# Windowed attention and a cosine MLP in one kernel: double bursts, a late division in the first chunk, and dues shifted by part

## The chip, the cores and the metric

The kernel runs on one core of a Trainium2 chip. A core has five engines that run side by side, each through its own list of instructions: TensorE (PE, with its weight loads shown as PEld), VectorE (DVE), ScalarE (ACT), GpSimd (POOL) and SyncE (SP, which issues the DMAs). They wait for each other by semaphores. The metric is the device time of one execution in microseconds (us); lower is better. Before the change the median of three runs is 677.84 us (677.83 to 678.22).

## The reference

Inputs are `q`, `k`, `v` of 4 batches, 8 heads, 768 positions, 64 numbers a head; a token sees the 96 positions up to itself and the first 8 (global) ones, with a bias that falls linearly with the distance at a slope of its head. The result goes through a two-layer network with `h * cos(h)` between.

```python
scores = scale * np.matmul(q, k.transpose(0, 1, 3, 2))
...
dist = np.where(is_global & ~is_local, float(n_local), np.abs(rel).astype(np.float32))
slopes = 2.0 ** (-8.0 * (np.arange(H, dtype=np.float32) + 1) / H)
scores = np.where(keep, scores - slopes * dist, -1e9)        # per head
a = np.exp(scores - np.max(scores, axis=-1, keepdims=True))
a = a / (np.sum(a, axis=-1, keepdims=True) + 1e-09)
x = np.matmul(a, v)                                          # 3072 tokens x 512
...
h = x @ w_in                                                 # 512 x 2048
return ((h * np.cos(h)) @ w_out).astype(np.float32)          # 2048 x 512
```

`w_in` and `w_out` arrive as 8-byte numbers and are taken apart on the chip into a high and a low 4-byte part; products of the network are made of three matmuls (high by high, low by high, high by low).

## The kernel before, in words

Work comes in chunks. Chunks 0 and 1 are the two halves of batch 0, four blocks of 96 positions each (OPEN). Batches 1 to 3 have three chunks each (BLOCKS): two of three blocks and one of two, chunks 2 to 10. Each chunk has four units, one for each pair of heads (UB is 1, so `plan_unit` and `plan_values` deal with one pair at a time).

A unit goes like this. Scores on PE (L678 where the unit is "exact", the eight units of chunks 0 and 1; L682 elsewhere) go into a PSUM bank. DVE folds two masked pieces into one (L700) and then, in one instruction for each block and head (L709), adds the distances `dd`, scales and keeps the maximum. ACT takes the exponential and its sum (L734). DVE adds 1e-9 and inverts the sums (L742, L745). POOL or DVE multiplies the probabilities by that inverse (`norm`, L762 and L767). PE turns them (L866), DVE and ACT copy them to `pv` (L877, L883, L310), and a burst of small matmuls (L917) multiplies them by the values into a bank `px`: each matmul writes one half of the partitions, a half for each head of the pair. Then `plan_x` copies `px` to the high part of x (`high`, L310 or L312) and subtracts for the low part (`rest`, L965). In an exact unit the queries are scaled by a factor of the head first (`queries`, L633 or L635, with the column `steep`), so that all heads can share one tile of distances.

`MERGE` names the chunks in which the units of an even and an odd pair share a burst; in this kernel it is empty, and only chunks of two blocks do so (`both`, L823). In a shared burst of more than two blocks each pair has its own `px` bank.

The network's first product is L1000, its second L1013 for chunks 0 to 2 and L1213 for the rest, between them a chain on ACT and DVE (L1018 to L1068).

Order is not that of the code. Every piece is an `Op` with the engines that may do it and an estimated cost; `Plan.run` plays the program forward and lets each free engine take, of the pieces that are ready, the one with the lowest key: the time at which it is due less its cost. What comes out is the list that each engine runs. `Op.name` begins with the part of the program that made it (`u3.1` is the unit of pair 1 of chunk 3, `s40` a step of the network, `wi5` a weight tile). `emit` (L1547) writes the lists, and where PE has a planned gap before 45 us it puts matmuls on zeros (L1572), here called fillers.

PSUM has eight banks: two for the network's first product, four for its second, and two for attention (class `att`); chunks 1 to 3 use three for attention, and chunk 0 all.

Of the kernel before, what the change touches and what calls it, by code (L numbers as in the profile page):

```python
# [21 lines left out]
P = 128  # L22
# [43 lines left out]

BEHIND = 0
MOE, AV = 348, 160
MERGE = tuple(range(11, 11))
DIFFER = tuple(range(4, 11))  # L70
COPIED = ()
APART = ()
BEFORE = {0: 4000, 1: 2500, 2: 25000}
WLEAD = -5000
SLACK = 350
TAIL = 0.8

ORDER = {}

FILL_TO, FILL_REST, FILL_EACH, FILL_FIRST, FILL_COLD = 45000, 150, 250, 10, 7000  # L80

# [30 lines left out]
class Plan:  # L112
# [54 lines left out]
    def run(self):  # L167

        self.dues()
        for i, o in enumerate(self.ops):  # L170
            o.key = (o.due - min(o.engines.values()) + ORDER.get(o.name, 0), i)
        ready = {e: [] for e in self.free}
        coming = []
        for o in self.ops:
# [111 lines left out]
class Net:  # L286
# [30 lines left out]
    def constants(self):  # L317
        nc = self.nc
        self.zeros = self.const.tile([P, P], BF16, name="zeros")
        nc.vector.memset(self.zeros, 0.0)  # L320

        first = self.const.tile([P, 1], F32, name="first")
        nc.scalar.activation(first, self.zeros[:, 0:1], AF.Exp)
        self.ident = self.const.tile([P, P], F32, name="ident")
        make_identity(nc, self.ident)
        tile3 = lambda name, **kw: self.const.tile([R, 3, SLOT], F32, name=name, **kw)


# [24 lines left out]
        self.own = self.const.tile([SLOT, R], F32, name="own")  # L353
        for x in (self.mine, self.own):
            g.memset(x, 1.0)
        keep(self.mine[:, 0, :], [[-1, R]], 1, 0.0)
        keep(self.own, [[1, R]], -1, 0.0)

        self.steep = self.const.tile([P, self.NP], F32, name="steep")
        for i in range(self.H):  # L360
            a = i % 2 * (P // 2)
            g.memset(self.steep[a : a + P // 2, i // 2 : i // 2 + 1], self.steepness(i))
        self.half_pi = self.const.tile([P, 1], F32, name="half_pi")
        g.memset(self.half_pi, math.pi / 2)
        self.worst = self.const.tile([P, 2 * CT], F32, name="worst")
        g.memset(self.worst, -3.0e38)
        self.words = self.const.tile([P, 4], U32, name="words")
        self.small = self.const.tile([P, 16], F32, name="small")
        self.ones = self.small[:, 10:11]
        g.memset(self.ones, 1.0)  # L370
        self.lim = self.small[:, 8:10]
        self.ngf, self.nlf = self.lim[:, 0:1], self.lim[:, 1:2]
# [5 lines left out]
    def plan_masks(self):  # L378
# [14 lines left out]
        def nearer(e):  # L393
# [14 lines left out]
        o = p.op({DVE: 400}, lambda e: v.scalar_tensor_tensor(  # L408
            self.dd, col, back[:R], keep, op0=ALU.min, op1=ALU.max), [o], use, port=True)
        self.masked = o  # L410


    def plan_weights(self, f):
# [191 lines left out]
    def plan_unit(self, L, pr):  # L605
# [16 lines left out]
        if exact:  # L622
# [4 lines left out]
            def load(e):  # L627
                nc.sync.dma_start(raw.tile[:, k0 : kw + wq], src[:, k0 : kw + wq])

            def queries(e):  # L630
                x = raw.tile[:, kw : kw + wq]
                if e == ACT:
                    nc.scalar.activation(x, x, AF.Copy, scale=self.steep[:, pr : pr + 1])  # L633
                else:
                    self.eng(e).tensor_scalar(x, x, self.steep[:, pr : pr + 1], 1.0, op0=ALU.mult, op1=ALU.mult)  # L635

            o = p.op({SP: 470}, load, [], [raw], extra=1422 * (kw + wq - k0) // 1000)
            ready = [p.op({ACT: 100 + wq * 420 // 384, DVE: 70 + wq * 230 // 384, POOL: 100 + wq * 390 // 384},
                          queries, [o], [raw], port=True)]
            heads = [(raw, ready)] * 2  # L640
        else:
            heads = [
# [21 lines left out]
        for job in jobs:  # L664
# [29 lines left out]
            for ps, items in pss:  # L694
# [8 lines left out]
                for i, (t, j) in enumerate(items):  # L703

                    def least(e, i=i, t=t, j=j, ps=ps):
                        w = width(t)
                        at = 2 * t + j
                        v = t if first and t < 2 else 2
                        nc.vector.tensor_tensor_reduce(  # L709
                            tt[t // 2].tile[:, t % 2, j, :w],  # L710
                            ps.tile[:R, i * WIN : i * WIN + w],
                            self.dd[:, v, :w],
                            op0=ALU.add,
                            op1=ALU.min,
                            scale=-(2.0 ** -(2 * pr + j + 1)),
                            scalar=3.0e38,
                            accum_out=st.tile[:, at : at + 1],
                        )

                    ttr.append(((t, j), p.op({DVE: 188}, least, [o, self.masked], [ps, tt[t // 2], st])))  # L720

        n2 = 2 * nb

# [25 lines left out]
        for ts in groups:  # L749
            h, na = ts[0], 2 * len(ts)  # L750
            if n in APART or ends is None:
                cs = (2 * h, 2 * h + na) if n in APART else (0, n2)
                ends = [x for ((t, _), _), x in zip(ttr, exps) if t in ts or n not in APART]
                o = p.op({DVE: 85}, lambda e, cs=cs: add(e, *cs), ends, [st], port=True)
                o = p.op({DVE: 120}, lambda e, cs=cs: rec(e, *cs), [o], [st], port=True)

            def norm(e, h=h, na=na):
                x = tt[h // 2].tile.rearrange("p t j w -> p (t j) w")[:, :na]
# [60 lines left out]
    def plan_values(self, u):  # L819
# [28 lines left out]
        for ts in u["groups"]:  # L848
# [46 lines left out]
            o = self.chain("pt", p.op({PE: 85 * na}, turn, [u["norm"][h // 2]], [pt, pv, tt[h // 2]]))  # L895
# [43 lines left out]
            [vd] * differ + list(dict.fromkeys(o for x in units for o in x[4])), mode="columns"))  # L939
        done.slack = SLACK if n not in EARLY else 0  # L940
        if n < len(OPEN):
            self.plan_x(n, pr, n, 0, px, 0, CW, done)
            return
        b, blocks = self.parts[n]
        s0 = b * self.S + blocks[0] * R
# [8 lines left out]
    def plan_x(self, n, pr, m, at, px, c0, w, done):  # L954

        nc, p = self.nc, self.plan
        xs = self.xs(m)
        a, c = slice(at, at + w), slice(c0, c0 + w)

        def high(e):  # L960
            self.copy(e, self.xtile(m)[0][:, pr, a], px.tile[:, c])
# [530 lines left out]
    def windows(self):  # L1492
# [11 lines left out]
                "rr": names("rr", NRR), "gg": names("gg", NG), "wu": names("late", 2), "late": names("late", 4),  # L1504
# [144 lines left out]
```

## Time and profile before

| what | us |
|---|---|
| median of three runs | 677.84 |
| the profiled execution | 677.51 |
| its span (first to last instruction) | 675.8 |
| PE busy | 663.6 |
| DVE busy | 551.4 |
| ACT busy | 504.9 |
| POOL busy | 393.0 |

Busy times are sums over the span and may hide stages with different limits; that of PE contains the fillers, and the ends of its matmuls are modelled, so that overlapping records count once. How fast PE really goes is read from the starts of its instructions. A row of the timeline merges instructions of one kind that follow each other: its first number is the start of the first, its second the time that they are busy, and `x` their number.

### The profile page before, as it was taken

How to read it: one execution, taken by the hardware profiler on the slowest of the kernel's cores; microseconds unless marked ns; L12 is line 12 of the kernel's file. 1: busy time of each engine (PE TensorE's matmuls, PEld its weight loads, DVE VectorE, ACT ScalarE, POOL GpSimd, SP SyncE). 2: the span in 40 equal slices, each digit the busy share in tenths (PEclk: the TensorE clock that was granted, in tenths of full speed). 3: DMA queues.
4: the chain of work that ended last, by engine and by line, in shares of the span. 5: the costliest groups of instructions: out<-in, count | busy, mean ns of one | idle time of the engine just before them, and what ended most of it. 6: DMA issues, size and time to landing. Idle time of an engine off the chain costs nothing.

```text
span 675.8 us, 17500 instructions
## 1 busy us (share of the span) xinstructions
PE 663.6 (98%) x5813; PEld 626.6 (93%) x5813; DVE 551.4 (82%) x1727; ACT 504.9 (75%) x1246; POOL 393.0 (58%) x576
## 2 busy tenths in 40 slices
PE   8999999999999999999999999999999999999995
PEld 4769999999999999999999999999999999999995
DVE  7999898978898998878788878876877887877664
ACT  7999997579776786866787779657777878684431
POOL 5896544447457553466667775757766867632201
PEclk9999999999999999999999999999999999999999
DMA  8999200044546767777878777876788677765663
GB/s 287 340 311 381 78 1 1 22 160 122 162 139 194 223 191 212 221 226 223 233 225 227 236 233 217 256 214 216 228 230 238 213 218 240 223 194 187 195 225 102
DMA packets 86003, 135.91 MB, mean 201 GB/s; under 512 B 9872, under 2 KB 34192, under 8 KB 85904
## 3 DMA queue, kind: packets, MB, share of 16 engines
q1 hardware_dynamic: 85760, 134.57, 65.0%
q8 instruction: 48, 0.79, 0.5%
q14 instruction: 51, 0.42, 0.2%
q10 hardware_dynamic: 144, 0.13, 0.1%
HBM read 117.88 MB, written 16.78 MB: 199 GB/s over the span
## 4 chain that ended last, share of the span: by engine, by line
PE 90%; DVE 4%; ACT 3%; issue 1%; DMA 1%; POOL 0%; SPq 0%; DVEq 0%; ACTq 0%; POOLq 0%
PE bank L1000 40%; PE bank L1213 22%; PE bank L1013 13%; PE bank L917 6%; PE bank L682 5%; PE bank L866 3%; ACT tt L734 1%; PE bank L678 1%; DVE tt L709 1%; DVE bank L700 1%; DMA raw<-in_qo_dram 1%; DVE sl L1174 0%; POOL tt L767 0%; DVE xmem L965 0%; PE bank L1288 0%
## 5 line engine op out<-in xcount | busy, mean ns | idle before, releaser
L1000 PE MATMUL bank<-xmem,w 128*128 128x256 f32 (+1 forms) x2112 | 345.0, 294 | 0.5 <-DVE rr L1057 0.4
L1000 PEld LDWEIGHTS bank<-xmem,w 128*128 128x128 f32 x2112 | 294.2, 188 | 8.4 <-DVE rr L1057 1.0
L734 ACT ACTIVATE tt<-tt,st 96x104 f32<-96x104 f32 (+1 forms) x256 | 94.5, 371 | 9.4 <-DVE st L709 8.7
L1013 PE MATMUL bank<-w,gh 128*128 128x256 f32 (+1 forms) x384 | 88.2, 320 | 0.0
L1024 ACT ACTIVATE rr<-rr,half_pi 128x512 f32<-128x512 f32 (+1 forms) x104 | 71.7, 692 | 21.3 <-DVE rr L1021 20.3
L1018 ACT ACTIVATE rr<-bank 128x512 int32<-128x512 f32 (+1 forms) x104 | 58.1, 560 | 30.7 <-PE bank L1000 28.8
L1213 PE MATMUL bank<-ws,sh 128*128 128x256 f32 x378 | 74.4, 283 | 0.0
L1021 DVE SCALAR_TENSOR_TENSOR rr<-rr,bank 128x512 f32<-128x512 int32 (+1 forms) x104 | 66.5, 639 | 8.2 <-ACT rr L1018 7.6
L767 POOL TENSOR_TENSOR tt<-tt,st 96x416 f32<-96x416 f32 (+1 forms) x60 | 44.2, 745 | 37.3 <-DVE qk L793 8.2
L803 POOL TENSOR_TENSOR qk<-raw,qk 64x304 fp32r<-64x304 f32 (+1 forms) x58 | 51.7, 893 | 22.3 <-DVE qk L793 6.0
L1013 PEld LDWEIGHTS bank<-w,gh 128*128 128x128 f32 x384 | 62.6, 188 | 1.1
L1057 DVE TENSOR_TENSOR rr<-bank,rr 128x512 f32<-128x512 f32 x72 | 49.3, 685 | 17.3 <-ACT rr L1024 17.1
L1013 PE MATMUL bank<-w,gl 128*128 128x256 f32 (+1 forms) x192 | 61.1, 318 | 0.0
L1213 PEld LDWEIGHTS bank<-ws,sh 128*128 128x128 f32 x378 | 57.7, 188 | 0.5 <-DVE oo L1242 0.2
L709 DVE CUSTOM_DVE_ANT_0 tt<-bank,dd 96x104 f32<-96x104 f32 (+1 forms) x256 | 55.4, 256 | 2.4
L310 ACT CAST gh<-rr 128x384 fp32r<-128x384 f32 (+1 forms) x74 | 38.6, 521 | 22.0 <-DVE rr L1057 12.6
L1213 PE MATMUL bank<-ws,sl 128*128 128x256 f32 x189 | 53.1, 281 | 0.1
L1024 ACT ACT_TABLE_LOAD x39 | 50.0, 1283 | 0.7
L682 PE MATMUL bank<-qk 128*96 128x200 f32 (+1 forms) x384 | 49.3, 257 | 0.3 <-DVE xmem L965 0.3
L700 DVE COPY_PREDICATED bank<-mine,bank 96x192 f32<-96x192 uint32 (+1 forms) x128 | 40.1, 328 | 11.2 <-PE bank L682 10.3
L734 ACT ACT_TABLE_LOAD x38 | 48.8, 1283 | 0.7
L459 POOL TENSOR_SCALAR raw<-raw 128x512 bf16<-128x512 bf16 (+1 forms) x32 | 35.6, 1135 | 23.3 <-DVE w L480 13.3
(140 smaller groups left out, 1543.5 us busy)
## 6 DMA issues: line engine op xcount, KB each, us to landing
ws<-sum SPq DMA_DIRECT2D x253, 256.0 KB
raw<-in_qk_dram SPq DMA_DIRECT2D x48, 174.0 KB
raw<-in_w_in_dram SPq DMA_DIRECT2D x16, 512.0 KB
sum<-sw SPq DMA_DIRECT2D x64, 128.0 KB
raw<-in_qk_dram SPq DMA_DIRECT2D x48, 150.0 KB
raw<-in_qk_dram SPq DMA_DIRECT2D x48, 148.0 KB
out_dram<-oo SPq DMA_DIRECT2D x23, 256.0 KB
raw<-in_w_out_dram SPq DMA_DIRECT2D x16, 256.0 KB
```

Of the source, the lines that this page charges most:

```text
L682: nc.tensor.matmul(out, qs[:, m, q0], ks[:, k : k + w], start=m == 0, stop=m == 1)
L700: nc.vector.copy_predicated(w[:, :, :R], self.mine.bitcast(U32).broadcast_to([R, ni - i0, R]), w[:, :, SLOT:])
L709: nc.vector.tensor_tensor_reduce(tt[t // 2].tile[:, t % 2, j, :w], ps.tile[:R, i * WIN : i * WIN + w], self.dd[:, v, :w], op0=ALU.add, op1 ...
L734: nc.scalar.activation(x, x, AF.Exp, bias=st.tile[:, c : c + 1], scale=-1.0, accum_out=st.tile[:, n2 + c : n2 + c + 1])
L803: self.eng(e).tensor_tensor(ks[D:, k0:k1], raw.tile[D:, k0:k1], ks.bitcast(F32)[D:, k0:k1], op=ALU.subtract)
L1000: self.nc.tensor.matmul(ph, self.wi[f][:, w, kk * P : (kk + 1) * P], xx[:, kk, :], start=kk == 0 and m == 0, stop=kk == self.NK - 1 and m ...
L1013: self.nc.tensor.matmul(out, gg, w[:, i, :], start=start and m == 0 and h == 0, stop=stop and m == 2)
L1018: self.nc.scalar.activation(r.bitcast(I32), ph, AF.Copy, scale=1.0 / TWO_PI, bias=0.25)
L1021: self.nc.vector.scalar_tensor_tensor(r, r.bitcast(I32), -TWO_PI, ph, op0=ALU.mult, op1=ALU.add)
L1024: self.nc.scalar.activation(r, r, AF.Sin, bias=self.half_pi)
L1057: {DVE: dve(512)}, lambda e: nc.vector.tensor_tensor(r(), h(), r(), op=ALU.mult), [o], [ph, rr],
L1213: nc.tensor.matmul(out, x, y, start=q == 0 and j == 0 and half == 0, stop=q == final and j == 2 and ends)
```

## The change

`MERGE` now holds chunks 2 to 10, so that in each of them pairs 0 and 1, and pairs 2 and 3, share a burst. `AFTER` holds chunk 0: its probabilities are not multiplied by the inverse sums before they are turned. Instead `plan_spread` lets PE spread the inverse sums over a bank of the same shape as `px` (8 matmuls a unit), ACT or DVE copies that bank to `xr`, DVE multiplies `px` by it, and the high and low part of x are made from the product, the low part on DVE or POOL. Instead of scaling queries, exact units have a distance tile for each head, `far`, made once from `dd` (8 instructions on DVE or POOL). And `ORDER` shifts the key of nearly every part's pieces by a number of its own.

```diff
-MERGE = tuple(range(11, 11))
+MERGE = tuple(range(2, 11))
+AFTER = (0,)
-ORDER = {}
+ORDER = {
+    "": 1376, "far0": -1384, "far1": 1802, "far2": 803, "far3": -6000, "far4": 351, "far5": 5735, "far7": -1212,
...
+}
-            o.key = (o.due - min(o.engines.values()) + ORDER.get(o.name, 0), i)
+            o.key = (o.due - min(o.engines.values()) + ORDER.get(o.name.split(" ")[0], 0), i)
...
+            def far(e, h=h, box=box):
+                self.eng(e).tensor_scalar(box(), self.dd, 2.0**-(h + 1) * math.sqrt(self.D), 1.0, op0=ALU.mult, op1=ALU.mult)
+            p.part = f"far{h}"
+            self.far.append((slot, box, p.op({DVE: 230, POOL: 400}, far, [o], [slot], port=True)))
...
-            ready = [p.op({ACT: 100 + wq * 420 // 384, DVE: 70 + wq * 230 // 384, POOL: 100 + wq * 390 // 384},
-                          queries, [o], [raw], port=True)]
+            ready = [o]
...
-                            self.dd[:, v, :w],
+                            (self.far[2 * pr + j][1]() if exact else self.dd)[:, v, :w],
-                            scale=-(2.0 ** -(2 * pr + j + 1)),
+                            scale=-1.0 / math.sqrt(D) if exact else -(2.0 ** -(2 * pr + j + 1)),
...
+            if n in AFTER:
+                u["sums"] = o
+                u["norm"].append([x for ((t, _), _), x in zip(ttr, exps) if t in ts])
+                continue
...
+    def plan_spread(self, u):
+        nc, p, D = self.nc, self.plan, self.D
+        nb, st = u["nb"], u["st"]
+        rb = self.bank(u["att"])
+        def spread(e):
+            for t in range(nb):
+                for j in range(2):
+                    c = 4 * nb + 2 * t + j
+                    nc.tensor.matmul(
+                        rb.tile[j * D : (j + 1) * D, t * R : (t + 1) * R],
+                        st.tile[:, c : c + 1].broadcast_to([R, D]), self.ident[:R, :R], start=True, stop=True)
+        return rb, p.op({PE: AV * nb}, spread, [u["sums"]], [st, rb], mode="columns")
...
+            rb, o = self.plan_spread(u)
+            xr = Slot("xr", lambda i: (self.const if i[0] == "w" else self.work).tile([P, CW], F32, name="xr", tag=i))
+            o = p.op({ACT: 50 + w * 427 // 512, DVE: 70 + w * 535 // 512},
+                     lambda e: self.copy(e, xr.tile, rb.tile[:, :w]), [o], [rb, xr])
+            o = p.op({DVE: 70 + w * 535 // 512}, lambda e: nc.vector.tensor_tensor(
+                xr.tile, px.tile[:, c], xr.tile, op=ALU.mult), [o, done], [px, xr])
...
```

The order that comes out is shown at three places. The names are those of the code; L954 in the changed kernel is L917 in the kernel before, L1071 is L1000, L1284 is L1213, L903 is L866, L709 is L678, L766 is L734 and L1644 is L1572. On PE, in chunk 8 (batch 3, blocks 0 to 2), around the burst of pair 1, before:

```order
L1213 MATMUL bank<-w,sh 128x256 x2
L1213 MATMUL bank<-w,sl 128x256
L1000 MATMUL bank<-xmem,w 128x256 x6
L917 MATMUL bank<-pv,v 64x96 x4
L917 MATMUL bank<-pv,vd 64x96 x2
L917 MATMUL bank<-pv,v 64x96 x2
L917 MATMUL bank<-pv,vd 64x96 x2
L1000 MATMUL bank<-xmem,w 128x256 x6
L1213 MATMUL bank<-ws,gh 128x256 x2
```

And on PE in chunk 8 around the burst that pairs 0 and 1 now share:

```order
L1284 MATMUL bank<-ws,sh 128x256 x2
L1284 MATMUL bank<-ws,sl 128x256
L954 MATMUL bank<-pv,v 64x96 x4
L954 MATMUL bank<-pv,vd 64x96 x2
L954 MATMUL bank<-pv,v 64x96 x2
L954 MATMUL bank<-pv,vd 64x96 x2
L954 MATMUL bank<-pv,v 64x96 x4
L954 MATMUL bank<-pv,vd 64x96 x2
L954 MATMUL bank<-pv,v 64x96 x2
L954 MATMUL bank<-pv,vd 64x96 x2
L1071 MATMUL bank<-xmem,w 128x256 x3
```

The matmuls of pair 0, which had a burst of their own earlier in the list, now stand directly ahead of those of pair 1. (A matmul of the list in L917 is two records in the trace.)

On PE in the opening, around the first burst of chunk 0, before:

```order
L866 MATMUL bank<-ident,tt 96x96 x2
L866 MATMUL bank<-ident,tt 104x96 x2
L678 MATMUL bank<-raw 96x96 x2
L678 MATMUL bank<-raw 96x200 x2
L1572 LDWEIGHTS zeros
L1572 MATMUL idle<-zeros 128x512
L1572 LDWEIGHTS zeros
L1572 MATMUL idle<-zeros 128x512
L917 MATMUL bank<-pv,v 64x96 x14
L866 MATMUL bank<-ident,tt 104x96 x4
```

And on PE around the first burst of chunk 0 now:

```order
L903 MATMUL bank<-ident,tt 104x96 x4
L709 MATMUL bank<-raw 96x200 x4
L903 MATMUL bank<-ident,tt 96x96 x2
L903 MATMUL bank<-ident,tt 104x96 x2
L954 MATMUL bank<-pv,v 64x96 x14
L903 MATMUL bank<-ident,tt 104x96 x4
L1644 LDWEIGHTS zeros
L1644 MATMUL idle<-zeros 128x512
L1644 LDWEIGHTS zeros
L1644 MATMUL idle<-zeros 128x512
L1001 MATMUL bank<-ident,st 64x96 x8
```

The spread (L1001) is new; two fillers that stood ahead of the burst stand ahead of the spread. In the whole list there are 35 fillers where there were 48.

On ACT at the program's start, before:

```order
L323 ACT_TABLE_LOAD
L323 ACTIVATE first<-zeros 128x1
L633 ACTIVATE raw<-raw,steep 128x384 x2
L734 ACTIVATE tt,st<-tt,st 96x96
L734 ACTIVATE tt,st<-tt,st 96x104
```

And on ACT at the program's start now:

```order
L352 ACT_TABLE_LOAD
L352 ACTIVATE first<-zeros 128x1
L766 ACTIVATE tt,st<-tt,st 96x96
L766 ACTIVATE tt,st<-tt,st 96x104
L766 ACTIVATE tt,st<-tt,st 96x96
```

The scalings of the queries are gone from ACT's list, so that the exponentials come first.

## Rows read from the trace of the kernel before

**Rows 1.** Page, part 1: busy us of each engine, share, instructions.

```profile
PE 663.6 (98%) x5813; PEld 626.6 (93%) x5813; DVE 551.4 (82%) x1727; ACT 504.9 (75%) x1246; POOL 393.0 (58%) x576
```

**Rows 2.** By stretch: us, busy PE, PEld, DVE, ACT, POOL, clock, DMA share, GB/s.

```profile
0.00:20.00 20.00, 17.95 (x139) 9.97 (x140) 15.20 (x97) 15.49 (x67) 11.41 (x43) 1.00 0.89 298
20.00:40.00 20.00, 19.30 (x209) 14.50 (x211) 18.82 (x86) 19.98 (x68) 17.58 (x19) 1.00 1.03 327
40.00:60.00 20.00, 19.32 (x182) 15.15 (x176) 19.13 (x73) 19.87 (x54) 16.64 (x23) 1.00 0.98 342
...
140.00:340.00 200.00, 199.99 (x1751) 190.36 (x1750) 168.83 (x554) 155.85 (x381) 114.93 (x163) 1.00 0.64 193
340.00:600.00 260.00, 258.24 (x2440) 252.53 (x2439) 207.68 (x672) 196.13 (x484) 181.60 (x270) 1.00 0.77 228
```

**Rows 3.** Busy time by stretch of the fillers alone: the sum over 0 to 60.

```profile
sum 60.00, PE 13.79; mean PE 2.76
```

**Rows 4.** Timeline of PE, 319.7 to 323.2: start, us, engine, line, operation, names, shape.

```profile
319.73 0.64 PE L1000 MATMUL bank<-xmem,w 128*128 128x256 f32 x4
320.21 0.40 PE L1213 MATMUL bank<-ws,gh 128*128 128x256 f32 x2
320.44 0.28 PE L1213 MATMUL bank<-ws,gl 128*128 128x256 f32 x1
320.56 0.51 PE L1000 MATMUL bank<-xmem,w 128*128 128x256 f32 x3
321.00 0.55 PE L917 MATMUL bank<-pv,v 96*64 96x96 f32 x8
321.38 0.34 PE L917 MATMUL bank<-pv,vd 96*64 96x96 f32 x4
321.55 0.34 PE L917 MATMUL bank<-pv,v 104*64 104x96 f32 x4
...
321.98 1.33 PE L1000 MATMUL bank<-xmem,w 128*128 128x256 f32 x9
323.15 0.29 PE L682 MATMUL bank<-qk 128*96 128x96 f32 x2
```

**Rows 5.** Timeline behind that burst: the copies of its bank.

```profile
322.14 0.45 ACT L310 CAST xmem<-bank 128x256 fp32r<-128x256 f32 x2
322.63 0.52 DVE L965 TENSOR_TENSOR xmem<-bank,xmem 128x256 fp32r<-128x256 f32 x2 [0.40 <-ACT xmem L310]
```

**Rows 6.** Page, part 5: scores of the later chunks; busy, mean, idle before, releaser.

```profile
L682 PE MATMUL bank<-qk 128*96 128x200 f32 (+1 forms) x384 | 49.3, 257 | 0.3 <-DVE xmem L965 0.3
```

**Rows 7.** Timeline of the opening, 5 to 13 us: mask, distances, query scaling, normalisation.

```profile
5.76 0.54 DVE L408 SCALAR_TENSOR_TENSOR dd<-tmp,small,tmp 96x312 f32<-96x312 f32 x1
6.87 0.25 DVE L709 CUSTOM_DVE_ANT_0 tt<-bank,dd 96x96 f32<-96x96 f32 x1
7.69 0.59 POOL L635 TENSOR_SCALAR raw<-raw,steep 128x384 f32<-128x384 f32 x1 [2.67 <-DVE bank L700]
11.06 0.99 POOL L762 TENSOR_TENSOR tt<-tt,st 96x192 f32<-96x192 f32 x2 [2.78 <-ACT tt L734]
12.22 0.88 POOL L767 TENSOR_TENSOR tt<-tt,st 96x416 f32<-96x416 f32 x1 [0.17 <-ACT tt L734]
```

**Rows 8.** Groups by line and shape: count, busy us, mean ns, idle before.

```profile
L1068 POOL TENSOR_TENSOR gl<-rr,gh 128x384 fp32r<-128x384 f32 x21 | 21.9, 1043 | 1.9 <-ACT gh L310 1.4 <-DVE qk L793 0.5
L965 DVE TENSOR_TENSOR xmem<-bank,xmem 128x384 fp32r<-128x384 f32 x8 | 4.4, 555 | 0.7 <-ACT xmem L310 0.5
L310 ACT CAST xmem<-bank 128x384 fp32r<-128x384 f32 x6 | 2.8, 466 | 0.0
```

**Rows 9.** The chain that ended last, pieces in 0 to 50 us: start, us, what.

```profile
5.08 0.62 ACT raw L633
12.52 0.51 ACT raw L633
...
49.56 1.73 POOL tt L767 x2
```

More of the change, by code (lines that the diff above doesn't have):

```diff
@@ L357, in constants @@
         keep(self.own, [[1, R]], -1, 0.0)
[L359 to L362, printed above, removed]
         self.half_pi = self.const.tile([P, 1], F32, name="half_pi")
@@ L410, in plan_masks @@
         self.masked = o
+        homes = ["dd0"] * 3 + ["dd1"] * 3 + ["dd2"] * 2
+        held = {}
+        self.far = []
+        for h, c in enumerate(homes):
+            if c not in held:
+                held[c] = Slot(c, lambda i: self.const.tile([R, 3, 3, SLOT], F32, name="far", tag=i))
+            slot, at = held[c], homes[:h].count(c)
+            box = lambda slot=slot, at=at: slot.tile[:, at]
+            def far(e, h=h, box=box):
+                self.eng(e).tensor_scalar(box(), self.dd, 2.0**-(h + 1) * math.sqrt(self.D), 1.0, op0=ALU.mult, op1=ALU.mult)
+            p.part = f"far{h}"
+            self.far.append((slot, box, p.op({DVE: 230, POOL: 400}, far, [o], [slot], port=True)))
     def plan_weights(self, f):
@@ L718, in least @@
                         )
-                    ttr.append(((t, j), p.op({DVE: 188}, least, [o, self.masked], [ps, tt[t // 2], st])))
+                    slot, _, made = self.far[2 * pr + j] if exact else (None, None, self.masked)
+                    ttr.append(((t, j), p.op({DVE: 188}, least, [o, made], [ps, tt[t // 2], st] + [slot] * exact)))
         n2 = 2 * nb
@@ L893, in whole @@
                 self.copy(e, pv.tile[:R, 1, : 2 * R], pt.tile[:R, : 2 * R])
-            o = self.chain("pt", p.op({PE: 85 * na}, turn, [u["norm"][h // 2]], [pt, pv, tt[h // 2]]))
+            o = self.chain("pt", p.op({PE: 85 * na}, turn, u["norm"][h // 2] if n in AFTER else [u["norm"][h // 2]], [pt, pv, tt[h // 2]]))
             w = (na - a) * R
@@ L941, in plan_values @@
         if n < len(OPEN):
-            self.plan_x(n, pr, n, 0, px, 0, CW, done)
+            self.plan_x(n, pr, n, 0, px, 0, CW, done, u if n in AFTER else None)
             return
@@ L952, in plan_values, with plan_x @@
                 s = end
-    def plan_x(self, n, pr, m, at, px, c0, w, done):
+    def plan_spread(self, u):
[10 more added lines that the diff above has]
+        return rb, p.op({PE: AV * nb}, spread, [u["sums"]], [st, rb], mode="columns")
+    def plan_x(self, n, pr, m, at, px, c0, w, done, u=None):
         nc, p = self.nc, self.plan
@@ L958, in plan_x, with low @@
         a, c = slice(at, at + w), slice(c0, c0 + w)
+        if u is not None:
+            rb, o = self.plan_spread(u)
[4 more added lines that the diff above has]
+                xr.tile, px.tile[:, c], xr.tile, op=ALU.mult), [o, done], [px, xr])
+            o = self.chain("xh", p.op(
+                {ACT: 50 + w * 475 // 512, DVE: 70 + w * 265 // 512, POOL: 100 + w * 490 // 512},
+                lambda e: self.copy(e, self.xtile(m)[0][:, pr, a], xr.tile), [o], [xr, *xs], port=True))
+            def low(e):
+                xh, xl = self.xtile(m)
+                self.eng(e).tensor_tensor(xl[:, pr, a], xr.tile, xh.bitcast(F32)[:, pr, a], op=ALU.subtract)
+            self.xdone.setdefault((m, pr), []).append(p.op(
+                {DVE: 70 + w * 535 // 512, POOL: 100 + w * 1125 // 512}, low, [o], [xr, *xs], due=self.xdue(n, pr), port=True))
+            return
         def high(e):
@@ L1503, in windows @@
                 "part": names("oo", NOO) + names("sf", 1), "x0": ["x0"], "x1": ["x1"], "x2": ["x2"], "vd": names("vd", 1), "pv": names("pv", NPV), "x": names("x", NX),
-                "rr": names("rr", NRR), "gg": names("gg", NG), "wu": names("late", 2), "late": names("late", 4),
+                "rr": names("rr", NRR), "gg": names("gg", NG), "wu": names("late", 2), "late": names("late", 4), "xr": names("vd", 1) + [f"wo{self.NF - 3}"],
+                "dd0": [f"wi{self.NF - 2}"], "dd1": [f"wo{self.NF - 1}"], "dd2": [f"wi{self.NF - 1}"],
                 "oo": names("oo", NOO), "sf": names("sf", 1), "str": [f"wo{f}1" for f in range(0, self.NF, 2)],
```

6 lines of the change are left out of this document (removed), and 26 rows, old and new, of the table ORDER.

## The prediction

> **What bounds the kernel now.** I read the page's busy shares first, then the busy time by stretch, then the chain that ended last, then single stretches of TensorE. The shares put PE at 98%, DVE at 82%, ACT at 75% [rows 1]. The table by stretch says where that average comes from [rows 2]. From 140 to 340 us PE is busy 199.99 of 200 us; from 340 to 600 it is busy 258.24 of 260, so it idles 1.8 us. In these stretches only less work on PE can shorten the kernel much; taking every visible idle moment out would give 1.8 us. The opening, 0 to 60 us, is another stage: DVE is busy 18.82 and 19.13 us of the two later slices of 20 us and ACT 19.98 and 19.87, and PE's own 97% there is partly filler, 13.8 us of matmuls on zeros that keep the engine active while it would wait [rows 3]. With 3.4 us of idle time (60 - 17.95 - 19.30 - 19.32), PE has 17.2 us of the first 60 to spare. So the opening is set by the vector engines, and the rest by the amount of work on PE.
>
> **Term 1, the double bursts (MERGE).** A burst is the run of small matmuls on L917 that multiplies the probabilities by the values; it writes the two halves of the partitions, so it uses the array in another shape than the matmuls around it. What it costs to go in and out is read from the burst at 321.00 us [rows 4]. Full-size matmuls there follow each other every 0.119 us (seven in 320.56 - 319.73 = 0.83). The three that stand before the burst take 321.00 - 320.56 = 0.44 instead of 0.36: 0.08 lost on entry. Inside the burst four records take 0.17 us, so its 20 take 0.83, but the burst lasts 321.98 - 321.00 = 0.98: 0.15 lost at its end. The nine matmuls behind it take 323.15 - 321.98 = 1.17 instead of 1.07: 0.10 lost on the way back. Together 0.33 us a burst, whatever its length. Before, there are 38 bursts: four pairs for each of the two opening chunks, 24 for the six chunks of three blocks, 6 for the three chunks of two blocks, where pairs are joined already. The change joins the 24 to 12, and the order of PE shows just that: eight rows of L954 with nothing between where four stood. The matmuls themselves are as many as before. 12 x 0.33 = 4.0 us less on PE, and all 12 lie behind 140 us, where PE is the bound: -4.0 us. From both sides: nothing, if the loss belongs to the change of the unit rather than of the shape, and -4.0, since no more than the whole loss can go.
>
> What can eat this: a double burst fills two PSUM banks at once, and from chunk 4 on the attention has only two (class "att"). Until one is copied out, the next scores cannot start. After the burst at 321.00 the copies of one pair start on ACT at 322.14 and end on DVE at 322.63 + 0.52 = 323.15, 1.2 us behind the burst's end [rows 5]; in the whole trace PE's scores wait once for such a copy, 0.3 us [rows 6]. TensorEngine Tiling (Array Packing) of the Trainium skill, PSUM Bottleneck, speaks against the change: packing speeds up TensorE but not the emptying of PSUM, which may become the limit. By the row the sum stays -4.0; by the rule the wait for the copies takes the place of the loss, and the sum would be 0 or above. I go by the row, and keep the rule's outcome as the third rival.
>
> **Term 2, the opening: division behind the values (AFTER), distances per head, no scaled queries.** Per engine, for the four units of chunk 0 and the eight exact units:
> - POOL loses four normalisations, 0.99 + 0.88 us each [rows 7], 7.5 us, and one query scaling of 0.59. It gains eight distance tiles "far": nearest rows are the same kind of instruction at 384 columns on POOL, 0.59 [rows 7], times 312/384 = 0.48, so 3.8 us; and four subtractions of 384 columns at 1.04 [rows 8], 4.2 us. Even: 8.1 out, 8.0 in.
> - ACT loses seven query scalings of 0.51 to 0.62 on the chain [rows 9], about 4 us, and gains four copies of the spread sums out of PSUM at 0.47 [rows 8], 1.9 us: -2 us.
> - DVE gets four multiplications of 384 columns that read PSUM in place of four subtractions of the same size at 0.56 [rows 8]: 0. Counted in the two programs, DVE's list up to the last masked multiplication of chunk 1 (the sixteenth on before's L883, the last thing before the last opening burst) has 253 instructions before and 253 now.
> - PE gains four spreads of 8 matmuls, which the trace shows as 16 records: 16 x 0.042 = 0.67 us, and three of the four stand alone and pay 0.33 more [rows 4]: 3.7 us. In exchange there are 35 fillers instead of 48. This lies in PE's 17.2 us of spare time, so I take 0; without that cover it costs 3.7.
>
> Latency: the first distance subtraction on DVE starts at 6.87, after the mask "dd" is done at 5.76 + 0.54 = 6.30 [rows 7]. Now a far tile stands between, 0.48 us on POOL with a hand-over: about 6.9 to 7.0, while DVE has three folds to do instead of two. 0 to +0.2, hidden. Waiting behind far on POOL are only the first weight conversions. The load queue now puts the first w_in tile (512 KB, 1.8 us at the 298 GB/s of the first slice [rows 2]) ahead of the fourth query tile; that unit's scores stand behind the first transposes in PE's list, so I count nothing, +0.5 at worst.
>
> What is on the chain that goes? Three query scalings, one of 0.62 and two of 0.51, 1.6 us [rows 9]; the first gives way to the mask, which ends later anyway. The normalisations that are on the chain (two pieces, the longer 1.73 at 49.56) belong to chunk 1, which keeps them. So dropping those of chunk 0 takes nothing off the chain directly. With DVE's list as long as before and DVE almost always busy, I take -0.5 of the -1.6, between +1 (spreads and copies late) and -4 (the whole 1.6 and the 2 us that ACT gets free).
>
> **Term 3, dues shifted by part (ORDER).** These numbers change when each piece stands in its engine's list, not what it costs. In the steady stretch they can win at most the 1.8 us that PE idles, and lose without a bound in the rows; the lists of PE show 9 to 15 full matmuls between the last transposes and a burst at most places, as before, so I take 0, from -1.8 to +4.
>
> **Sum.** -4.0 - 0.5 + 0 = -4.5 us. The profiled execution took 677.51 (span 675.8 and 1.7 around it), which becomes 673.0; the median of the three runs is 677.84, 0.3 above it, and I forecast 673.3 in its terms.
>
> **Rivals.**
> Forecast: the bursts pay in full, the opening gives little: 673.3, own range 671 to 675.8. Chance 0.56.
> Second, the opening shrinks too. ACT is lighter by 2 us, and the first burst's transposes no longer wait for 1.9 us of POOL. If chunk 0 is done that much sooner and DVE finds its idle time of 0 to 20 us (4.8 us [rows 2]) filled, PE is full of real work about 4 us sooner: 677.84 - 4.0 - 4 = 669.8. Against: the 253 DVE instructions, and DVE's 95% in 20 to 60 us. Chance 0.22.
> Third, slower: the banks. Two pairs need twice the 1.2 us of one to be copied out, 2.4 us if ACT and DVE are free at once [rows 5], and behind four of the eight double bursts that have only two banks PE's list holds under 3 us of full matmuls (15 or 24 of 0.119) before the next scores. If every double burst costs PE a wait w, the time is 677.84 - 4.0 - 0.5 + 12w. The gain is gone at w = 0.38, it is slower than the bound below from w = 0.5, and at w = 0.7 it is 681.7. Against: one bank, the first copied, is enough to go on, the copies are as many as before, and before has that one wait [rows 6]. Chance 0.08 for slower, 0.04 for about even.
> Fourth, the change doesn't do what it says: the loss of 0.33 belongs to the change of operands inside the burst, not to entering and leaving, and only the opening moves: 677.3. Chance 0.10, of which 0.06 within the bound.
>
> **How the numbers follow.** 0.2% is 1.4 us; a measurement of this kernel can tell no less from no change. Faster, below 676.5: 0.56 + 0.22 + 0.04 = 0.82. Within: 0.04 + 0.06 = 0.10. Slower, above 679.2: 0.08. The range leaves out the deepest part of the second rival and the third with the fourth: 669.4 to 677.4. The likeliest case gives 673.3.
>
> **What would show it.** Right: 26 bursts in the trace, those of chunks 2, 3, 5, 6, 8, 9 with 40 or 48 records and about 1.8 or 2.1 us long, PE's busy time down by about 4 us beside the fillers, the last opening burst still near 60 us, PE idle 1 to 3 us between 140 and 660. The opening is wrong if the last burst of chunk 1 stands 2 us or more off 60. The steady term is wrong if PE shows waits for copies into "xmem" behind the bursts, or if the matmul after a double burst comes later by more than the 0.15 and 0.10 above. The whole is wrong if PE idles more than 6 us behind 140.

## The result, and the profile after

The changed kernel takes 671.38 us (median of four runs, 671.14 to 671.66) where the kernel before took 677.85 beside it: 0.9903 of the time, 95% interval 0.9886 to 0.9921. The forecast was 673.3, with 669.4 to 677.4 as its range. The profiled executions took 671.51 and 677.51, with spans of 669.8 and 675.8. In the changed kernel L954 is the burst, L1071 and L1284 the network's products, L713 the scores, L1644 the fillers.

PE, page part 1 of the changed kernel, against [rows 1]: busy 5.0 us less. The fillers take 2.4 us less (11.36 against 13.79 [rows 3]), but the spreads, which are new, take 3.5. Between 0 and 60 us PE is busy 0.6 us longer than before, behind 60 us 5.6 us less.

```profile
PE 658.6 (98%) x5864; PEld 627.6 (94%) x5864; DVE 551.5 (82%) x1729; ACT 503.8 (75%) x1252; POOL 390.9 (58%) x558
```

```profile
sum 60.00, PE 11.36 PEld 3.34; mean PE 3.79 PEld 1.11
```

Busy time by stretch of the changed kernel (columns as in [rows 2]):

```profile
0.00:20.00 20.00, 17.46 (x174) 11.09 (x176) 15.93 (x100) 13.67 (x61) 9.56 (x34) 1.00 0.91 284
20.00:40.00 20.00, 19.87 (x233) 15.03 (x229) 18.86 (x89) 18.76 (x68) 14.84 (x17) 1.00 1.01 335
40.00:60.00 20.00, 19.83 (x181) 15.29 (x182) 19.08 (x67) 19.87 (x56) 15.72 (x23) 1.00 1.02 336
...
140.00:340.00 200.00, 198.49 (x1740) 190.39 (x1739) 170.30 (x552) 155.21 (x384) 131.14 (x177) 1.00 0.64 192
340.00:600.00 260.00, 259.85 (x2501) 256.94 (x2501) 214.56 (x707) 206.43 (x503) 165.42 (x237) 1.00 0.78 232
```

PE idles 1.66 us between 140 and 600, 1.77 before: the bound is the same, there is less to do. Where the work went shows in the timeline of PE in the changed kernel around a double burst of 40 records, against [rows 4]:

```profile
340.44 1.47 PE L1071 MATMUL bank<-xmem,w 128*128 128x256 f32 x11
341.83 0.55 PE L954 MATMUL bank<-pv,v 96*64 96x96 f32 x8
...
342.55 0.34 PE L954 MATMUL bank<-pv,vd 96*64 96x96 f32 x4
342.72 0.50 PE L954 MATMUL bank<-pv,v 96*64 96x96 f32 x8
...
343.38 0.33 PE L954 MATMUL bank<-pv,vd 96*64 96x96 f32 x4
343.65 0.62 PE L1071 MATMUL bank<-xmem,w 128*128 128x256 f32 x3
344.11 0.40 PE L1284 MATMUL bank<-w,gh 128*128 128x256 f32 x2
```

The entry still costs 0.08 (11 matmuls in 341.83 - 340.44 = 1.39 instead of 11 x 0.119 = 1.31) and the way back 0.10 (three in 0.46 instead of 0.36). The burst lasts 343.65 - 341.83 = 1.82, where two single ones lasted 0.98 each: 0.14 saved, since between its halves (342.55, 342.72) the step is 0.17 as everywhere inside. So a joined burst saves 0.08 + 0.14 + 0.10 = 0.32 us, and twelve 3.9.

To find the rest I took the starts of all matmuls: where an interval behind 62 us is clearly longer than is usual for the same three neighbours (line and shape) in the two traces, the excess is counted as a wait. That is a computation on the records, not a view, and its sums can move by up to 1 us with the threshold from which an excess counts. PE's waits fell from 5.7 to 4.3 us (with another threshold, from 6.6 to 4.3). From the start of the last opening burst to PE's last matmul the changed kernel takes 5.3 us less (608.5 to 603.2), so that 3.0 to 3.9 of it are less work. The start of that burst comes 0.37 earlier (60.04 to 59.67), and what follows PE's end takes 0.3 less. These three, 5.3, 0.37 and 0.3, make the 6.0 by which the spans differ.

### The profile page after: what moved, and what is told of

Same layout as the page of the kernel before. It is cut to its first block, busy times and chain, and to the rows that moved or that the text cites. A ratio compares the mean times of both kernels' runs of the same rounds, so it can differ in the third digit from the quotient of the medians.

```text
span 669.8 us, 17562 instructions
## 1 busy us (share of the span) xinstructions
PE 658.6 (98%) x5864; PEld 627.6 (94%) x5864; DVE 551.5 (82%) x1729; ACT 503.8 (75%) x1252; POOL 390.9 (58%) x558
## 4 chain that ended last, share of the span: by engine, by line
PE 85%; DVE 6%; ACT 3%; DMA 2%; issue 2%; POOL 1%; SPq 0%; DVEq 0%; POOLq 0%; ACTq 0%
PE bank L1071 37%; PE bank L1284 23%; PE bank L1084 11%; PE bank L954 5%; PE bank L713 5%; PE bank L903 3%; DVE tt L740 1%; ACT tt L766 1%; DMA raw<-in_qk_dram 1%; DVE bank L731 1%; PE bank L1001 0%; PE bank L709 0%; DMA words<-in_lim_dram 0%; POOL sw L550 0%; DVE rr L1092 0%
## 5 line engine op out<-in xcount | busy, mean ns | idle before, releaser
L1071 PE MATMUL bank<-xmem,w 128*128 128x256 f32 (+1 forms) x2112 | 330.3, 294 | 1.1 <-DVE rr L1128 0.9
L1071 PEld LDWEIGHTS bank<-xmem,w 128*128 128x128 f32 x2112 | 290.1, 188 | 7.1 <-issue 1.3
L766 ACT ACTIVATE tt<-tt,st 96x104 f32<-96x104 f32 (+1 forms) x256 | 94.5, 370 | 9.4 <-DVE st L740 8.8
L1284 PE MATMUL bank<-ws,sh 128*128 128x256 f32 x378 | 72.7, 282 | 0.0
L804 POOL TENSOR_TENSOR tt<-tt,st 96x416 f32<-96x416 f32 (+1 forms) x56 | 42.0, 755 | 42.5 <-DVE sw L550 6.2
L840 POOL TENSOR_TENSOR qk<-raw,qk 64x304 fp32r<-64x304 f32 (+1 forms) x54 | 49.6, 922 | 24.4 <-ACT tt L766 4.5
L1284 PEld LDWEIGHTS bank<-ws,sh 128*128 128x128 f32 x378 | 57.7, 188 | 0.0
L1284 PE MATMUL bank<-ws,sl 128*128 128x256 f32 x189 | 53.0, 280 | 0.0
L498 POOL TENSOR_SCALAR raw<-raw 128x256 bf16<-128x256 bf16 (+1 forms) x30 | 30.8, 1059 | 33.7 <-DVE wu L509 10.7
L339 ACT CAST gh<-rr 128x384 fp32r<-128x384 f32 (+1 forms) x70 | 36.1, 517 | 19.2 <-PE bank L1284 12.5
L713 PE MATMUL bank<-qk 128*96 128x200 f32 (+1 forms) x384 | 49.5, 255 | 0.1
L1284 PE MATMUL bank<-w,gh 128*128 128x256 f32 x252 | 49.0, 283 | 0.0
```

The costliest lines, as they stand in the source:

```text
L713: nc.tensor.matmul(out, qs[:, m, q0], ks[:, k : k + w], start=m == 0, stop=m == 1)
L766: nc.scalar.activation(x, x, AF.Exp, bias=st.tile[:, c : c + 1], scale=-1.0, accum_out=st.tile[:, n2 + c : n2 + c + 1])
L804: self.eng(e).tensor_tensor(x, x, r.broadcast_to([R, na, SLOT]), op=ALU.mult)
L840: self.eng(e).tensor_tensor(ks[D:, k0:k1], raw.tile[D:, k0:k1], ks.bitcast(F32)[D:, k0:k1], op=ALU.subtract)
L1071: self.nc.tensor.matmul(ph, self.wi[f][:, w, kk * P : (kk + 1) * P], xx[:, kk, :], start=kk == 0 and m == 0, stop=kk == self.NK - 1 and m ...
L1284: nc.tensor.matmul(out, x, y, start=q == 0 and j == 0 and half == 0, stop=q == final and j == 2 and ends)
```

## The experiments

In all of them the kernel before ran beside: 677.72, 677.55 and 677.93 us in the three groups. Median times and PE's waits behind 62 us, computed as above ("the dues" or "the table" is `ORDER`):

| kernel | us | ratio to before | PE's waits |
|---|---|---|---|
| before | 677.85 | 1 | 5.7 |
| changed | 671.38 | 0.9903 [0.9886, 0.9921] | 4.3 |
| e1_break | 674.73 | 0.9952 [0.9936, 0.9969] | 4.3 |
| e2_same | 672.37 | 0.9927 [0.9905, 0.9949] | 3.5 |
| e12_spread2 | 673.32 | 0.9936 [0.9922, 0.9949] | 3.3 |
| e4_merge_alone | 681.91 | 1.0056 [1.0035, 1.0078] | 13.6 |
| e10_opendues | 687.14 | 1.0131 [1.0101, 1.0162] | 19.2 |
| e14_after_noport | 689.74 | 1.0162 [1.0141, 1.0182] | 18.5 |
| e5_nomerge | 689.86 | 1.0190 [1.0171, 1.0210] | 16.6 |
| e6_noafter | 690.05 | 1.0187 [1.0170, 1.0204] | 16.4 |
| e8_dues_alone | 699.87 | 1.0323 [1.0302, 1.0343] | 24.1 |
| e11_steadydues | 718.80 | 1.0609 [1.0591, 1.0627] | 48.6 |
| e3_noorder | 727.10 | 1.0741 [1.0700, 1.0781] | 55.1 |
| e13_noorder_noport | 741.01 | 1.0939 [1.0904, 1.0974] | 68.7 |

**Is it the change of shape?** Two kernels with the changed kernel's lists and one addition between the halves of each of the twelve double bursts, a full-size matmul on zeros (e1) or two half-partition ones (e2), into an unused part of the bank.

```diff
+                if i == 0 and len(units) == 2 and nb == 3:
+                    nc.tensor.matmul(unit[6].tile[:, 3 * R : 3 * R + P], self.zeros, self.zeros, start=True, stop=True)
```

e1 was expected so: 

> The changed kernel, with one full-size matmul on zeros (128 columns, bf16) between the two pairs of each of the 12 double bursts, into columns of the bank that nobody reads; all lists are otherwise the same. Theory (the 0.33 us is paid for entering and leaving the half-partition shape): each insertion costs 0.33 plus some 0.06 for the matmul, 12 x 0.39 = 4.7 us, 676.1 us, and the trace shows the pair before and after it 0.4 us further apart. Rival (the loss belongs to the change of the unit and is paid inside the double burst already): only the matmuls, 12 x 0.06 = 0.7, 672.1 us.

e2, with two matmuls of the half shape there: 

> The changed kernel, with two half-partition matmuls on zeros (128 columns, bf16, one for each half) at the same 12 places. Both theories: the shape is not left, so only the matmuls are paid, 12 x 0.06 to 0.11 = 0.7 to 1.3 us, 672.1 to 672.7 us. If this costs 3 us or more, the insertion itself is what costs, and the other experiment tells nothing.

Timeline of PE in e1 around the same burst:

```profile
343.34 0.55 PE L954 MATMUL bank<-pv,v 96*64 96x96 f32 x8
...
344.06 0.34 PE L954 MATMUL bank<-pv,vd 96*64 96x96 f32 x4
344.32 0.23 PE L974 MATMUL bank<-zeros 128*128 128x128 bf16 x1
344.48 0.55 PE L954 MATMUL bank<-pv,v 96*64 96x96 f32 x8
...
345.46 0.62 PE L1073 MATMUL bank<-xmem,w 128*128 128x256 f32 x3
```

And in e2:

```profile
342.04 0.55 PE L954 MATMUL bank<-pv,v 96*64 96x96 f32 x8
...
342.93 0.23 PE L975 MATMUL bank<-zeros 128*64 128x128 bf16 x2
...
343.92 0.62 PE L1074 MATMUL bank<-xmem,w 128*128 128x256 f32 x3
```

With the full shape inside, the burst lasts 2.12 us, with the half shape 1.88, without either 1.82. The burst's length again shows the shape: 0.24 us for leaving and coming back, 12 x 0.24 = 2.9, and the medians of e1 and e2 differ by 2.36. That is somewhat less than 0.32, and e1 ended at 674.73 instead of the 676.1 expected. e2 changes operands at the same place as e1, without the shape, and costs 0.06 a burst (1.0 us in the medians); so the rival (the loss belongs to the operands) falls.

**The joined bursts without the dues.** The kernel before with `MERGE` alone.

```diff
-MERGE = tuple(range(11, 11))
+MERGE = tuple(range(2, 11))
```

> The kernel before with joined bursts from chunk 2 on, nothing else. Theory (the bursts pay in full, PE being the bound): 677.85 - 4.0 = 673.9 us, give or take 1 for the new lists. Rival (two banks held at once make PE wait for the copies unless the dues are shifted): 677.9 us or more, with waits of PE for copies into xmem behind the bursts.

It is 4.2 us slower than before. What PE waited for behind 62 us, by the view of waits (us in total, times, longest):

```profile
PE bank L1000 <- DVE rr L1057: 1.9, 4, 0.6
PE bank L866 <- POOL tt L767: 1.2, 2, 0.9
PE bank L682 <- DVE qk L793: 1.0, 1, 1.0
```

The rival's time is met, its mechanism (banks) isn't: no copy into `xmem` is among the waits of this view, which are 6.0 us in all, the part of the 13.6 in which PE stands idle; and followed by the semaphores of each late matmul, waits for such a copy make up 0.1 us of the 13.6. Joining makes the burst wait for the later pair and moves its matmuls; the plan reshuffles every list, and the network's chain, the normalisations and the splitting of queries come late in turn. How the one leads to the other was not traced. Its waits of 13.6 us are 7.9 more than before's, twice what joining saves.

**The dues taken away.** The changed kernel with `ORDER = {}`.

> The changed kernel with an empty ORDER: joined bursts, late division and distances per head, dues unshifted. Theory (the measured 6.5 us are 4.0 of the bursts and some 2 of a better order, since PE's waits behind 60 us fell): 673.4 us or more, with PE idle longer in the steady stretch or the last opening burst later than 59.7. Rival (the dues are worth nothing, all comes from the edits): 671.4 us within 0.7.

The rival failed, and of the first theory only the open end ("or more") held, not its size of some 2 us: 727.1 us. One wait is 30.7 of the 55.7 us that it lost against the changed kernel. PE and then GpSimd in e3, by their timelines (the last bracket: idle before, and for what):

```profile
98.83 1.40 PE L875 MATMUL bank<-ident,tt 96*104 96x96 f32 x6 [30.66 <-POOL tt L776]
```

```profile
97.73 1.89 POOL L776 TENSOR_TENSOR tt<-tt,st 96x416 f32<-96x416 f32 x2 [38.74 <-DVE sw L522]
```

VectorE in the meantime, by line and shape (count, busy us, mean ns, idle before), in 66 to 97 us:

```profile
L491 DVE TENSOR_TENSOR w<-wu,w 128x512 fp32r<-128x512 f32 x18 | 12.1, 695 | 0.0
L481 DVE SCALAR_TENSOR_TENSOR wu<-raw 128x512 uint32<-128x512 uint32 x17 | 11.6, 700 | 0.0
L467 DVE TENSOR_SCALAR raw<-raw 128x512 uint16<-128x512 uint16 x13 | 9.7, 742 | 0.0
```

It was never idle. VectorE's list has 46 weight conversions in a row here, and the plan put the normalisation, whose inputs were ready at 59.24 (end of the inversion, L749), behind them. In the changed kernel's list at most 9 follow each other, in before's 7. In lists made without dues (not run) the row is 46 long with single bursts too, but only 4 or 5 without late division, or with scaled queries: it takes both edits of the opening.

Then half of the dues. The table without the entries of chunks 2 to 10 and of steps from s16 on: 

> The changed kernel with the shifted dues of the opening's parts alone (far, weights, wo and wi, the sums c, units of chunks 0 and 1, network steps s0 to s15); the dues of chunks 2 to 10 and of steps 16 on are unshifted. First theory, the dues of the steady stretch are worth only the wait that the changed kernel's trace shows less than before's, 1.5 to 2 us: 673 to 674 us. Rival, the joined bursts need the shifted dues of the later chunks, without them PE waits some 8 us more behind 140 us as in the kernel before with joined bursts alone (681.9): 679 us or more.

The table with those entries alone: 

> The changed kernel with the shifted dues of chunks 2 to 10 and steps 16 on alone; the opening's parts are unshifted. In its list VectorE has no long row of weight conversions (the one of 46 in a row that stood ahead of a normalisation when all dues were unshifted is not there). First theory, that row was the whole of the stall of 30.7 us: 671 to 674 us. Rival, the opening needs its own dues: a wait of several us in 60 to 140 us, 680 us or more.

The premise of e11's expectation was wrong: its list has the row of 46 as well. It kept the long wait (30.6 us), so it is the opening's own dues that break the row up, and with the steady half in place PE's waits behind 300 us are 4.0 us, against 14.6 in e3. In e10 the rival holds: it lost 15.8 us, nearly all of it as waits (14.9 more than the changed kernel). Two of the largest in e10:

```profile
PE bank L886 <- POOL tt L787: 2.0, 3, 0.9
...
PE bank L1054 <- DVE rr L1111: 1.3, 3, 0.6
```

Transposes wait for normalisations, the network's product for its chain: as in e4, the joined bursts without fitting dues.

**One edit taken back, or one alone.** The changed kernel with `MERGE` empty: 

> The changed kernel with MERGE empty (every pair its own burst again; late division, distances per head and shifted dues kept). First theory, prices that add up: 12 bursts more at 0.34 us each, the saving that the changed kernel's trace shows, so 671.4 + 4.1 = 675.5 us (675 to 676), with PE's waits behind 60 us as in the changed kernel. Rival, the dues are numbers for one list: without the joined bursts they fit no more, and PE's waits grow by several us as they did when the bursts were joined in the kernel before, so 678 us or more.

With `AFTER` empty: 

> The changed kernel with AFTER empty: chunk 0 divides its probabilities before they are turned, as in the kernel before; everything else kept. First theory, the late division is worth no more than the 0.4 us by which the last opening burst came earlier: 671.4 to 672.4 us, last opening burst at 59.7 to 60.5. Rival, it opened the first burst 3.7 us earlier and so carries the opening: last opening burst 62 or later and 674 us or more. A third, it costs (seven kinds of work for one): 670.5 or less.

And the kernel before with the table alone: 

> The kernel before with the table of shifted dues alone (names split as in the changed kernel): single bursts, division ahead of the transposes, scaled queries. By prices that add up, the dues take 1.5 to 2 us of PE's waits behind 60 us: 676 us. By the theory that the table fits one list only, PE waits longer than in the kernel before, by as much as in the changed kernel without joined bursts or without late division (12 us): 685 us or more.

The sums of prices missed by 14, 18 and 24 us, and the rivals hold. The waits grew by 12.3 (e5) and 12.1 (e6) over the changed kernel's, and by 18.4 (e8) over before's. In e5 the opening is as in the changed kernel (its last burst at 59.64), and the waits come behind 140 us. The largest:

```profile
PE bank L1071 <- DVE rr L1128: 4.4, 5, 1.4
```

In e6 it is the opening that comes late. Its last burst, by PE's timeline (the changed kernel's starts at 59.67):

```profile
69.45 1.55 PE L954 MATMUL bank<-pv,v 104*64 104x96 f32 x32
```

and its largest wait, which lies between 60 and 140 us:

```profile
PE bank L1071 <- DVE rr L1194: 4.3, 2, 2.5
```

So 9.8 of the 17.4 us by which e6's span is longer are there when the last opening burst starts, and both signs of its rival came true (62 or later, 674 or more). In e8 that burst starts at 68.26, against 60.04 in the kernel before. All three agree with the theory that the table fits one set of edits. It is not shown that the plans in between need a table at all: no other order was tried for them. What late division is worth by itself can't be had from e6, whose plan differs everywhere; the kernel before divides early too, under its own order, and has its last opening burst at 60.04.

**Is PE's filler time spare?** The changed kernel with its four spreads issued twice, all lists otherwise the same.

```diff
-            for t in range(nb):
+            for t in [*range(nb), *range(nb)]:
```

> The changed kernel with the matmuls of each of the four spreads issued twice into the same place; plan, order and fillers as they are. 64 records more at 0.042 us, 2.7 us more on PE in the first 45 us. First theory, they lie in PE's spare time in the opening: 671.4 us within 0.5, last opening burst at 59.7. Rival, PE's work in the opening is on the path: 673 to 674.1 us, last opening burst at 61 or later.

The last opening burst in the changed kernel, by PE's timeline:

```profile
59.67 1.55 PE L954 MATMUL bank<-pv,v 104*64 104x96 f32 x32
```

In e12:

```profile
62.24 1.55 PE L954 MATMUL bank<-pv,v 104*64 104x96 f32 x32
```

It moved by 2.57 us, nearly the whole of the 2.7 added, and the time rose by 1.9. The rival holds: once the fillers stand in PE's list they take their time like work. What was spare for the plan is not spare for the list. Whether the opening would be shorter without fillers was not tried.

**Who holds GpSimd back?** The kernel makes each GpSimd instruction wait for the VectorE instruction on the shared port that the plan put ahead of it. Without that wait, all lists the same, in e3 and in the changed kernel:

```diff
-                    self.tc.add_manual_dep(new[0], held_by.name, behind, reason="port")
```

> The changed kernel without shifted dues, as in e3_noorder (727.1 us), but GpSimd's instructions do not wait for the VectorE instruction that the plan put ahead of them on the shared port; the order of every engine's list is the same, and data is waited for as before. First theory, the stall of 30.7 us is that wait: the normalisation stood behind 46 weight conversions only in the plan, so it starts near 59.4 us instead of 97.7, the wait of PE shrinks to under 3 us, and the time is 695 to 700 us. Rival, VectorE's conversions, one on the heels of the other, keep GpSimd out of the port by themselves: the normalisation still starts behind 75 us, PE waits 15 us or more, 711 us or more.

> The changed kernel with the same waits of GpSimd for VectorE's place on the port taken out and nothing else changed: every list is the same. First theory, in the changed kernel's list these waits cost PE nothing that can be seen, since none of its waits over 0.2 us is for a GpSimd instruction held by them: 671.4 us within 1. Rival, the two engines run into each other on the port, VectorE's or GpSimd's instructions get longer than in the changed kernel (busy 551 and 391 us), and PE waits for them: 674 us or more. Third, GpSimd starts earlier and PE's waits shrink: 670 us or less.

GpSimd's normalisation in e13:

```profile
63.21 3.82 POOL L776 TENSOR_TENSOR tt<-tt,st 96x416 f32<-96x416 f32 x2 [3.08 <-DVE st L749]
```

and PE's wait:

```profile
106.91 1.37 PE L926 MATMUL bank<-pv,v 104*64 104x96 f32 x12 [32.13 <-DVE pv L886]
```

Each theory was half right, at 741.0 us. GpSimd did start right behind the inversion, as the first has it, so the planned wait was what held it in e3. But PE's wait and the time are the rival's: the burst waited 32.1 us for copies to `pv` on VectorE, which stand behind the same conversions. So VectorE's list is enough for the stall by itself, and GpSimd's wait in e3 was one sign of it. In e14 the rival holds, at 18.4 us: the same lists, longer instructions (below). Its last opening burst starts at 66.14, so that 6.5 us of them are lost by then.

## Why the prediction was right, and where it was not

- **Term 1, -4.0.** Right in mechanism and size: 26 bursts, 40 records in 1.82 us, 3.9 by the timeline. e1 shows that the shape is what costs, at 0.24 of the 0.33 when it is put back. The whole stretch behind the last opening burst lost 3.0 to 3.9 us of work, as computed above; whether other transitions of the list took some back was not traced. The sign "PE's busy time down by about 4 us beside the fillers" was a poor one: it is down 2.6 beside them, with the new spreads in it, and 6.0 without the spreads. But "from both sides: nothing, and -4.0" left out the other side: by the plan of before joining costs 4.2 us (e4).
- **The rule on PSUM.** TensorEngine Tiling (Array Packing) of the Trainium skill, PSUM Bottleneck, says that the copies may become the limit. The trace does not bear this out here: the scores' line has 0.1 us of idle time in all, against the 0.3 of [rows 6], though the copies behind the burst shown run to 345.97, 2.3 us past its end, as rival three had it. PE had full matmuls meanwhile. Page part 5 and VectorE's timeline of the changed kernel:

```profile
L713 PE MATMUL bank<-qk 128*96 128x200 f32 (+1 forms) x384 | 49.5, 255 | 0.1
```

```profile
345.55 0.42 DVE L1036 TENSOR_TENSOR xmem<-bank,xmem 128x256 fp32r<-128x256 f32 x1
```

- **Term 2, -0.5.** The last opening burst came 0.37 earlier, right in size. It is the size of this opening under this table only: with late division taken back the same burst comes 9.8 us later (e6). The estimates of the new pieces held (mean ns, by line and shape, changed kernel; estimated 1040, 480, 560 and 470):

```profile
L1025 POOL TENSOR_TENSOR xmem<-xr,xmem 128x384 fp32r<-128x384 f32 x4 | 4.0, 1001 | 0.0
L446 POOL TENSOR_SCALAR far<-dd 96x312 f32<-96x312 f32 x8 | 3.5, 448 | 3.1 <-DVE dd L433 2.7
L1017 DVE TENSOR_TENSOR xr<-bank,xr 128x384 f32<-128x384 f32 x4 | 2.2, 553 | 0.6 <-PE bank L954 0.3 <-ACT raw L488 0.3
L339 ACT COPY xr<-bank 128x384 f32<-128x384 f32 x4 | 1.8, 474 | 0.1
```

  The cover was named too loosely. "PE's 17.2 us of spare time" hides a spread only as far as the plan gives up fillers for it, as it did here (48 to 35, 2.4 us); added to finished lists, nearly all of it counts (e12), so the vector engines alone do not set the opening.
- **Term 3, taken as 0, from -1.8 to +4: the step that failed.** The waits fell by 1.4 (by the looser count 2.3), so the sum came out 2 us too high and no worse. But the reading was wrong: I priced the dues as a correction of the steady stretch, beside edits that have their own prices. Under this table those edits are paid out, and in no other plan tried. With all edits and no dues 727.1; with half the table 687.1 or 718.8; with the table and one edit missing 690. Before has 5.7 us of waits under its own order, the changed kernel 4.3 under its table, and every other plan tried has 13.6 or more. I had the two lists to compare, and read from them how many matmuls stand ahead of a burst; that reading could not have told e10 from the changed kernel: in both, 12 or 15 stand ahead of most bursts behind 140 us. That the sum held is owed to the table, which I priced at nothing; that part was luck.
- **Rivals.** The second (the opening shrinks by 4) fails on the 0.37, though its premise came true: chunk 0's last burst starts 4.57 us sooner. The first burst of chunk 1, which keeps its early division, starts only 0.49 sooner (38.80 to 38.31). Before, and then the changed kernel:

```profile
31.46 1.39 PE L917 MATMUL bank<-pv,v 96*64 96x96 f32 x28
```

```profile
26.89 1.39 PE L954 MATMUL bank<-pv,v 96*64 96x96 f32 x28
```

  The third fails on L713. The fourth fails on e1. That an edit pays only under an order made for it was not among the rivals; as a forecast for this change it would have changed nothing, for the two parts tried alone (bursts, table) it would have turned the sign.

Why before's own order suits single bursts, scaled queries and early division so well, which entries of the table do the work, and whether another table would do for the plans in between, is open. Neither distances per head nor late division was tried alone.

## What to carry to other kernels

Where a planner writes the lists, the price of an edit is the work it removes plus the waits of the list that comes out, and the second part can be larger than the first: here it was two and three times the 4 us of the bursts (e4, e5). Judge such an edit together with its order, and test its own price by an addition that leaves the lists alone (a matmul more, an instruction twice). Of a long wait, look past the engine that is named for what stands ahead in the list of the one behind it.

## What the hardware showed that was not expected

Two engines on one port lengthen each other. In e13 the two normalisations of 96x416 shown above take 2.53 and 1.32 us, against 0.88 alone [rows 7]. The conversions on VectorE beside them:

```profile
65.05 1.25 DVE L491 TENSOR_TENSOR w<-wu,w 128x512 fp32r<-128x512 f32 x1
```

```profile
66.22 1.56 DVE L491 TENSOR_TENSOR w<-wu,w 128x256 fp32r<-128x256 f32 x1
```

The first took 0.695 on average in e3 (above), the second, of half the size, 0.44. In e14 the lists are those of the changed kernel, but VectorE is busy 584.5 us instead of 551.5 and GpSimd 414.0 instead of 390.9. By shape, the changed kernel:

```profile
L1202 DVE TENSOR_TENSOR gl<-rr,gh 128x384 fp32r<-128x384 f32 x22 | 14.6, 670 | 2.5 <-POOL gh L343 2.3 <-ACT gh L339 0.2
...
L804 POOL TENSOR_TENSOR tt<-tt,st 96x416 f32<-96x416 f32 x32 | 28.5, 895 | 31.9 <-DVE sl L1245 4.5 <-DVE sf L1238 3.6 <-DVE qk L830 3.2
```

and e14:

```profile
L1202 DVE TENSOR_TENSOR gl<-rr,gh 128x384 fp32r<-128x384 f32 x22 | 21.2, 969 | 2.6 <-POOL gh L343 1.9 <-ACT gh L339 0.6
...
L804 POOL TENSOR_TENSOR tt<-tt,st 96x416 f32<-96x416 f32 x32 | 32.7, 1029 | 28.2 <-DVE st L777 16.2 <-DVE st L740 5.2 <-ACT rr L1089 2.7
```

SBUF — State Buffer of the Trainium skill, Who interferes with whom, says that the pair of ports that VectorE and GpSimd share is an exclusive lock, and that a VectorE instruction with two SBUF inputs contends for it with a GpSimd instruction that reads SBUF. The rows agree with that, for both engines. That waiting on purpose is 18.4 us cheaper than letting them collide is e14's number, with these lists; a lower granted clock, 0.96 on average between 60 and 100 us, has a part in it.

TensorE's clock fell during e3's stall. By stretch (us, busy PE, granted clock, DMA share, GB/s):

```profile
64.00:68.00 4.00, 4.00 (x27) 1.00 1.05 399
68.00:72.00 4.00, 0.17 (x1) 0.81 1.06 203
72.00:76.00 4.00, 0.00 (x0) 0.50 0.48 137
...
106.00:110.00 4.00, 2.33 (x8) 0.50 0.76 263
110.00:114.00 4.00, 4.00 (x21) 0.82 0.00 0
```

A granted clock of 1.00 is the level of 2.4 GHz, 0.50 that of 1.2. PE went idle at 68, worked again from 98.83 with waits, and got the upper level back only between 110 and 114; a burst of 32 records took 2.85 us on the way, 1.55 at the upper level (above):

```profile
100.48 2.85 PE L926 MATMUL bank<-pv,v 104*64 104x96 f32 x32
```
